# Block 0's prologue: the root per half on GpSimd, the silu table first, both halves' products ahead of later rounding, the order written down

## The chip, the cores and the metric

The kernel runs on one core of a Trainium2 chip. The core has five engines that run on their own and meet at semaphores: TensorE (PE) multiplies, VectorE (DVE) and ScalarE (ACT) work elementwise, GpSimd (POOL) does elementwise work on SBUF, and SyncE (SP) issues most of the transfers. The metric is device time in microseconds, lower is better.

## The reference

Two layers, one behind the other. The first is attention without a softmax: for each of 8 batches and 8 heads, `kv = k^T v` over 576 positions, then `out = q kv`, and each 64-wide row of `out` is divided by its root mean square and multiplied by `g_norm`. The second is a gated feed-forward layer over 4608 tokens of width 512, with an inner width of 1536.

```python
kv = np.einsum('bhsd,bhse->bhde', k, v)
out = np.einsum('bhsd,bhde->bhse', q, kv)
rms = np.sqrt(np.mean(out * out, axis=-1, keepdims=True) + 1e-06)
out = out / rms * g_norm                      # -> x, 4608 x 512
g = x @ w_gate
silu = g * (1.0 / (1.0 + np.exp(-g)))
return silu * (x @ w_val) @ w_out
```

Inputs `q`, `k`, `v` and the output are float32; the three weight matrices arrive as 64-bit numbers, read as pairs of 32-bit words, and are made into float32 on the chip.

## The kernel before

The tokens are worked in nine blocks of 512. For each block, an `Att` object turns `q`, multiplies it by the `kv` of its batch, takes the root mean square, scales and turns the result into `x` (features on partitions); an `Ffn` object makes the gate and value products, `h = silu(g) * v`, and the down product. Blocks 1 to 8 use products with fewer multiplications, whose extra operands VectorE and GpSimd make; block 0 uses plain products (`plain_up`, twelve steps f = 0 to 11, each with four gate and four value matrix products), since its weights are still arriving.

The weights come in 36 pieces of 512 KB: gate and value in turn, twelve each, then twelve of `w_out`. A piece is a `Words` object. It is loaded into one of four buffers named `ld` by an SP transfer (L135). `begin` makes the magnitude of the high words on ScalarE (L146), clamps it (L147), masks out the sign (L152) and joins the two (L153), all three on VectorE; `finish` scales the low words on ScalarE (L160) and adds them in on VectorE (L162). `weights(n)` brings the count of rounded pieces to n, and each one asks for the load of a piece four ahead, which waits until a buffer is read out: by L152 and L160, the last readers of `raw`.

Block 0 starts in `first()`. The first two q tiles are turned on TensorE (L337) and copied out (L339 on ScalarE, L341 on VectorE); `first_kv` makes `kv` of batch 0 in two groups (L248) and copies and adds the banks (L253, L111); `heads` multiplies (L361); `squares` squares on ScalarE (L374) and sums on VectorE (L375). `root` takes the root of both halves in one go, on VectorE: a scaled sum (L381), a first guess from the bits (L384), and three refinement steps of three instructions each (L391 to L393). `warm` repeats a product that nobody reads, seven times (L496). `scale` multiplies a half by the root (L113), `turn_x` turns it on TensorE (L410) and copies it out with the gain on ScalarE (L411). A half is 256 tokens.

The order on each engine's queue comes from a scheduler that works through the program with costs and priorities; `tc.issue_after(x)` puts what stands under it behind instruction x. A queue is then worked strictly in that order. So a step that waits holds up what stands behind it on its engine.

After block 0's twelve steps, block 1's inputs are loaded by SP: `load_kv` (L266) and `load_q`, 32 small transfers (L284) into two `ld` buffers, once rounding has left these. VectorE turns q of block 1 (L331), and TensorE, after the first step of the down product (L565), multiplies it (L361). Silu is at L1040, the plain products at L1035.

Of the kernel before, what the change touches and what calls it, by code (L numbers as in the profile page):

```python
# [1 line left out]

# [16 lines left out]
def kernel(  # L19
# [41 lines left out]
    nc = tc.nc  # L61

    B, H, S, D = q.shape
# [7 lines left out]
    NS = DM // P  # L71
    NF = FF // P
# [3 lines left out]
    eps = 1e-6  # L76
# [6 lines left out]
    consts = pool("consts", 1)  # L83
    ld_pool = pool("ld", 4)
    st_pool = pool("st", 2)
# [26 lines left out]
    sub = lambda e, o, a, b: e.tensor_tensor(out=o, in0=a, in1=b, op=OP.subtract)  # L112
    mul = lambda e, o, a, b: e.tensor_tensor(out=o, in0=a, in1=b, op=OP.mult)  # L113

    def ring():

        return r_pool.tile([P, 4, BLK], F32, name="r")

    class Words:
# [12 lines left out]
        def __init__(self, src, shape):  # L132
            self.raw = ld_pool.tile([P, LD], U32, name="ld")[:, 0 : 2 * BLK]
            dst = self.raw.rearrange("p (a b) -> p a b", a=shape[0])
            self.sent = nc.sync.dma_start(out=dst, in_=src)  # L135
            self.shape = shape
            self.begun = False

        def begin(self):

            self.begun = True
            halves = self.raw.rearrange("p (f w) -> p f w", w=2)
            low, high = halves[:, :, 0], halves[:, :, 1]
            self.low, self.room = low, ring()
            mag = self.mag = self.room[:, 1].bitcast(U32)
            nc.scalar.activation(out=mag.bitcast(F32), in_=high.bitcast(F32), func=ACT.Abs)  # L146
            nc.vector.tensor_scalar(  # L147
                out=mag.bitcast(F32), in0=mag.bitcast(F32), scalar1=self.LOW, scalar2=self.HIGH,
                op0=OP.max, op1=OP.min,
            )  # L150
            sign = self.room[:, 2].bitcast(U32)
            nc.vector.tensor_scalar(out=sign, in0=high, scalar1=0x80000000, scalar2=None, op0=OP.bitwise_and)  # L152
            return nc.vector.scalar_tensor_tensor(  # L153
                out=mag, in0=mag, scalar=3, in1=sign, op0=OP.logical_shift_left, op1=OP.bitwise_xor
            )

        def finish(self, dst):

            unit = self.room[:, 0]
            nc.scalar.activation(out=unit, in_=self.low, func=ACT.Copy, scale=2.0**-51, bias=2.0)  # L160
# [32 lines left out]
    class Att:  # L193
# [128 lines left out]
                for r in range(2):  # L322
                    nc.scalar.copy(out=dst[:, r], in_=self.kv_ps[r])

        def turn_q(self, i, pools=None):

            if i == 0:
                self.qt = ring().rearrange("p j (t c) -> p t j c", t=T)
            if self.quarters:
                to = self.qt[:, :, 2 * i : 2 * i + 2].rearrange("p t j c -> p j t c")  # L330
                self.q_turned = nc.vector.transpose(out=to.rearrange("p j t c -> p (j t c)"), in_=self.q[i])  # L331
                return
            for t in (2 * i, 2 * i + 1):
                pool = pools[t % 2] if pools else m_psum
                ps = pool.tile([P, NS, P], F32, name=pool.name[0])
                for j in range(NS):
                    nc.tensor.transpose(ps[:, j], self.q[t][:, j], ident)  # L337
                if t % 2 if self.n == 0 else t:
# [127 lines left out]
        def first(self):  # L466
            self.turn_q(0, (b_psum, c_psum))
            self.first_kv(0, (b_psum, c_psum))
            last = self.first_kv(1, (b_psum, a_psum))

            with tc.issue_after(last.ins):
                self.heads(0, (0, 1), (m_psum, m_psum))
            with tc.issue_after(self.multiplied.ins):
                self.heads(0, (2, 3))
            self.squares(0)
            with tc.issue_after(self.multiplied.ins):
                self.turn_q(1, (b_psum, c_psum))

            with tc.issue_after(self.copied_q.ins), tc.issue_after(self.summed.ins):
                begun = words[pieces[0]].begin()  # L480
            with tc.issue_after(begun.ins):
                self.product(1, (b_psum, a_psum))
            self.warm()
            self.root(0, 2)
            self.scale(0)
            with tc.issue_after(self.squared.ins), tc.issue_after(self.scaled.ins):
                weights(1)
            self.turn_x(0)
            self.scale(1)
            return self.squared, self.scaled  # L490

        def warm(self):

            ps = c_psum.tile([P, NS, P], F32, name="c")
            for _ in range(7):
# [446 lines left out]
    class Ffn:  # L942
# [82 lines left out]

        def plain_up(self, f, halves=(0, 1)):

            if 0 in halves:
                self.ps[f] = [pool.tile([P, 2, HB], F32, name=pool.name[0]) for pool in (b_psum, c_psum)]
            of = slice(halves[0], halves[-1] + 1)  # L1030
            ps = [t[:, of] for t in self.ps[f]]
            x = self.att.x[:, 0:4].rearrange("p (h m) i t -> p (m i) h t", h=2)
            for t, w in zip(ps, (wg, wv)):
                for i in range(NS):
                    nc.tensor.matmul(  # L1035
                        t, lhsT=w[f // 2][:, i, P * (f % 2) : P * (f % 2 + 1)], rhs=x[:, i, of],
                        start=(i == 0), stop=(i == NS - 1),
                    )
            h = self.h[:, f].rearrange("p (h t) -> p h t", h=2)[:, of]
            nc.scalar.activation(out=h, in_=ps[0], func=ACT.Silu)  # L1040
            mul(nc.vector, h, h, ps[1])
# [37 lines left out]
    blocks[0].load_q(1)  # L1079
    load_weights(4)  # L1080
    squared, scaled = blocks[0].first()

    for n in range(NB):
        ffn = Ffn(n, blocks[n])
        nxt = blocks[n + 1] if n + 1 < NB else None
        if n == 0:

            with tc.issue_after(squared.ins), tc.issue_after(scaled.ins):
                weights(2)
            ffn.plain_up(0, (0,))  # L1090
            copied = blocks[0].copied
            blocks[0].turn_x(1)
            for f in range(NF):
                with tc.issue_after(blocks[0].copied.ins if f else copied.ins):
                    weights(2 * (f + 2))
                ffn.plain_up(f) if f else ffn.plain_up(0, (1,))
            weights(len(pieces))
            pairs = wo.rearrange("p (j e) d -> p e j d", e=2)
            t2(pairs[:, 0, :, HD:DM], pairs[:, 1, :, HD:DM], pairs[:, 0, :, 0:HD])
            nxt.room = x_pool.tile([P, 3, 7, P], F32, name="xi").rearrange("p a b c -> p (a b c)")  # L1100

            with tc.issue_after(sent.ins):
                for i in range(2):
                    nxt.load_kv(i)
                for i in range(2):
                    nxt.load_q(i)
            ffn.plain_end()
            for g in range(2):
                nxt.kv(g)
        else:  # L1110

            def visit(g):
                with tc.issue_after(ffn.multiplied.ins):
                    nxt.kv(g)
                if nxt.n < B:
                    ffn.visited = nxt.positions

            def third():
                visit(0)
# [12 lines left out]
            ffn.up(fill)  # L1132
# [48 lines left out]
```

## Time and profile before

| what | us |
|---|---|
| median of 3 runs (1021.38 to 1022.99) | 1022.85 |
| profiled execution | 1020.91 |
| its span, first to last instruction | 1019.1 |
| TensorE busy | 1003.5 |
| VectorE busy | 700.9 |
| GpSimd busy | 368.9 |
| ScalarE busy | 228.1 |

The span is what the trace covers; the profiled execution's own time is 1.8 us more. An engine's busy time counts its instructions, not its waits. TensorE is busy nearly all the time, and the chain that ended last runs over it for 90% of the span; VectorE holds 6% of that chain, transfers 2%, ScalarE 1%. The start of this chain, in order of time (start, length, what):

```profile
0.74 4.10 DMA h<-in_k_dram
4.85 0.02 issue
4.86 0.37 SPq L230
5.23 0.04 issue
5.28 7.74 DMA h<-in_v_dram
13.02 0.14 issue
13.15 0.37 PE b L248 x2
```

The first group's k and v arrive by 10 us and the second group's v at 13.02; until then loads set the pace. What the change touches lies behind that.

### The profile page before, as it was taken

The page shows a single profiled execution, that of the slowest core. Times are in us where ns is not written, and L with a number is a line of the kernel's source. Part 1 is how long each engine was busy: PE and PEld are TensorE (multiplying, and loading weights), DVE is VectorE, ACT ScalarE, POOL GpSimd, SP SyncE. Part 2 cuts the span into 40 slices and gives each one's busy share as a digit, 9 for nine tenths or more (in the row PEclk, how much of TensorE's full clock was granted, in tenths as well). Part 3 has the DMA queues.
Part 4 walks back from the last instruction along what each step waited for, and adds up shares of the span by engine and source line. Part 5 has one row for each costly group of instructions (what it writes and reads, how often), then busy time and mean ns, then how long its engine had stood idle before and what let it go on. Part 6 is the DMA issues. An engine that isn't in the chain of part 4 may idle for free.

```text
span 1019.1 us, 21397 instructions
## 1 busy us (share of the span) xinstructions
PE 1003.5 (98%) x8522; PEld 895.9 (88%) x8522; DVE 700.9 (69%) x1169; ACT 228.1 (22%) x353; POOL 368.9 (36%) x280
## 2 busy tenths in 40 slices
PE   6999999999999999999999999999999999999998
PEld 4544688888999899998999899988998999989997
DVE  3999688998666946685558566665668466946661
ACT  2765112121211221221121111111121211221110
POOL 0000263534055503561246315630555045513670
PEclk9999999999999999999999999999999999999999
DMA  8689643767888277846685568646772766066601
GB/s 238 202 257 273 119 81 109 188 165 159 251 231 244 50 195 202 248 83 147 206 234 136 101 207 241 168 62 194 233 201 44 182 191 192 22 169 199 194 25 42
DMA packets 273844, 170.26 MB, mean 167 GB/s; under 512 B 150608, under 2 KB 241872, under 8 KB 273744
## 3 DMA queue, kind: packets, MB, share of 16 engines
q1 hardware_dynamic: 238800, 164.42, 59.1%
q10 hardware_dynamic: 34880, 4.46, 2.7%
q8 instruction: 68, 1.11, 0.5%
q14 instruction: 32, 0.26, 0.1%
q0 software_dynamic: 64, 0.00, 0.0%
HBM read 138.02 MB, written 22.41 MB: 157 GB/s over the span
## 4 chain that ended last, share of the span: by engine, by line
PE 90%; DVE 6%; DMA 2%; issue 1%; ACT 1%; SPq 0%; DVEq 0%; ACTq 0%
PE b L728 26%; PE b L565 19%; PE c L728 13%; PE c L565 10%; PE a L728 6%; PE a L565 5%; PE b L1035 4%; PE c L1035 4%; PE m L361 1%; PE m L316 1%; DVE r L112 1%; DVE r L111 1%; DVE xi L112 1%; DMA h<-in_v_dram 1%; DVE t L112 1%
## 5 line engine op out<-in xcount | busy, mean ns | idle before, releaser
L111 POOL TENSOR_TENSOR r<-r 128x256 f32<-128x256 f32 (+1 forms) x105 | 110.7, 1061 | 295.2 <-DVE r L111 292.9
L111 DVE TENSOR_TENSOR r<-b,r 128x512 f32<-128x512 f32 (+1 forms) x273 | 161.9, 605 | 64.9 <-PE b L728 60.4
L112 POOL TENSOR_TENSOR t<-wo 128x512 f32<-128x512 f32 x81 | 114.4, 1436 | 211.9 <-DVE wo L111 102.6
L111 DVE TENSOR_TENSOR r<-c,r 128x512 f32<-128x512 f32 (+1 forms) x179 | 108.3, 616 | 89.1 <-PE c L728 58.2
L728 PE MATMUL b<-x,t 128*128 128x128 f32 x1092 | 151.2, 275 | 0.0
L111 DVE TENSOR_TENSOR r<-a,r 128x512 f32<-128x512 f32 (+1 forms) x99 | 62.4, 630 | 113.1 <-PE a L565 71.2
L728 PEld LDWEIGHTS b<-x,t 128*128 128x128 f32 x1092 | 136.5, 192 | 0.8 <-DVE r L111 0.2
L728 PE MATMUL c<-xi,t 128*128 128x128 f32 x840 | 112.4, 275 | 1.0 <-DVE xi L111 1.0
L113 POOL TENSOR_TENSOR h<-r 128x1024 f32<-128x1024 f32 (+1 forms) x40 | 82.4, 2075 | 82.2 <-DVE r L111 79.2
L728 PEld LDWEIGHTS c<-xi,t 128*128 128x128 f32 x840 | 102.9, 192 | 1.2 <-DVE xi L111 1.2
L565 PE MATMUL b<-wo,h 128*128 128x256 f32 x432 | 100.1, 383 | 0.1
L565 PE MATMUL b<-t,h 128*128 128x256 f32 x432 | 96.2, 379 | 0.0
L565 PEld LDWEIGHTS b<-t,h 128*128 128x128 f32 x432 | 82.0, 190 | 11.3 <-issue 0.2
L565 PEld LDWEIGHTS b<-wo,h 128*128 128x128 f32 x432 | 79.8, 190 | 13.2 <-DVE h L113 2.5
L742 ACT COPY r<-b 128x512 f32<-128x512 f32 x63 | 36.9, 585 | 214.9 <-PE b L728 208.1
L728 PE MATMUL b<-xi,t 128*128 128x128 f32 x588 | 79.7, 276 | 0.0
L728 PEld LDWEIGHTS b<-xi,t 128*128 128x128 f32 x588 | 72.4, 192 | 0.0
L728 PE MATMUL b<-x,wg 128*128 128x128 f32 x336 | 52.8, 279 | 0.2 <-DVE x L112 0.2
L728 PE MATMUL b<-x,wv 128*128 128x128 f32 x336 | 51.2, 275 | 0.0
L565 PE MATMUL a<-wo,h 128*128 128x256 f32 x216 | 48.3, 379 | 0.0
L565 PE MATMUL c<-t,s 128*128 128x256 f32 x216 | 48.1, 379 | 0.0
L565 PE MATMUL c<-wo,h 128*128 128x256 f32 x216 | 48.1, 379 | 0.0
(133 smaller groups left out, 1562.2 us busy)
## 6 DMA issues: line engine op xcount, KB each, us to landing
t<-w SPq DMA_DIRECT2D x336, 256.0 KB, 3.5
out_dram<-r SPq DMA_DIRECT2D x17, 512.0 KB, 3.1
ld<-in_k_dram SPq DMA_DIRECT2D x26, 288.0 KB, 4.9
ld<-in_v_dram SPq DMA_DIRECT2D x26, 288.0 KB, 5.8
ld<-in_moe_w_gate_dram SPq DMA_DIRECT2D x12, 512.0 KB, 4.7
ld<-in_moe_w_val_dram SPq DMA_DIRECT2D x12, 512.0 KB, 4.6
ld<-in_moe_w_out_dram SPq DMA_DIRECT2D x12, 512.0 KB, 5.0
w<-t SPq DMA_DIRECT2D x18, 256.0 KB, 3.0
```

The lines of the kernel that those rows point to most:

```text
L111: add = lambda e, o, a, b: e.tensor_tensor(out=o, in0=a, in1=b, op=OP.add)
L112: sub = lambda e, o, a, b: e.tensor_tensor(out=o, in0=a, in1=b, op=OP.subtract)
L113: mul = lambda e, o, a, b: e.tensor_tensor(out=o, in0=a, in1=b, op=OP.mult)
L316: self.positions = nc.tensor.matmul(self.kv_ps[r][u * D : (u + 1) * D, g, :], lhsT=k[:, u, c, :], rhs=v[:, u, c, :], start=(c == 0), stop= ...
L361: self.multiplied = nc.tensor.matmul(self.ps[i][u][p : p + D, t, j, :], lhsT=self.qt[rows, 2 * i + t, j, p : p + D], rhs=kvs[b % 3][rows, ...
L565: self.ffn.multiplied = nc.tensor.matmul(banks[e][:, e], lhsT=lhsT, rhs=rhs, start=first and i == 0 and (e == 0 or banks[0] is not banks[1 ...
L728: self.ffn.multiplied = nc.tensor.matmul(ps[:, i, f], lhsT=self.weight(o, p, f), rhs=self.operand(o, p), start=first and (i, f) == (0, 0), ...
L742: nc.scalar.copy(out=dst, in_=ps)
L1035: nc.tensor.matmul(t, lhsT=w[f // 2][:, i, P * (f % 2) : P * (f % 2 + 1)], rhs=x[:, i, of], start=(i == 0), stop=(i == NS - 1),)
```

## The change

The change rewrites block 0's prologue. Nine things are done:

- A small silu at the very start makes ScalarE load the silu's table there; the other functions used are in that table too, so the load ahead of the first real silu goes.
- `root` is no longer used by block 0. Each half has its own `inverse`: one VectorE instruction for the scaled sum, then GpSimd raises it to the power -0.5 with a constant tile `power`.
- `begin` is cut into `split` (magnitude, clamp, sign) and `join`; `scale` of the low words can be issued earlier. For the first two pieces VectorE masks the magnitude out as well, in place of ScalarE's L146.
- Both copies of the second pair of turned q tiles go to ScalarE.
- The second half's `heads` come before the first half's root is needed; `warm` has five repeats in place of seven.
- The first two pieces' steps are placed by hand between the halves' squares, sums and scales.
- TensorE's queue has half 0's gate and value products of f = 0, then half 1's turning, then half 1's products, where before the turning of half 1 was split around the value product.
- The third and fourth pieces (`weights(3)`, `weights(4)`) and the silus of f = 0 are put behind the last copy of x and the last scale.
- `in_order` writes the program's order down: each traced instruction of an engine is made to follow the one before it on that engine.

```diff
+    power = consts.tile([P, 4 * NS], F32, name="power")
+    nc.gpsimd.memset(power, -0.5)
+    early = consts.tile([P, 1], F32, name="early")
+    nc.vector.memset(early, 0.0)
+    nc.scalar.activation(out=early, in_=early, func=ACT.Silu)
...
         def begin(self):
             self.begun = True
+            self.split()
+            return self.join()
...
+        def split(self, engine=None):
...
+            if engine is nc.vector:
+                bits(sign, 0x80000000)
+                bits(mag, 0x7FFFFFFF)
+            else:
+                nc.scalar.activation(out=mag.bitcast(F32), in_=high.bitcast(F32), func=ACT.Abs)
...
         def first(self):
             self.turn_q(0, (b_psum, c_psum))
             self.first_kv(0, (b_psum, c_psum))
...
+            with in_order():
+                self.first_kv(1, (b_psum, a_psum))
                 self.heads(0, (0, 1), (m_psum, m_psum))
-            with tc.issue_after(self.multiplied.ins):
                 self.heads(0, (2, 3))
-            self.squares(0)
-            with tc.issue_after(self.multiplied.ins):
-                self.turn_q(1, (b_psum, c_psum))
-
-            with tc.issue_after(self.copied_q.ins), tc.issue_after(self.summed.ins):
-                begun = words[pieces[0]].begin()
-            with tc.issue_after(begun.ins):
-                self.product(1, (b_psum, a_psum))
-            self.warm()
-            self.root(0, 2)
-            self.scale(0)
-            with tc.issue_after(self.squared.ins), tc.issue_after(self.scaled.ins):
+                first.split(nc.vector)
+                self.square(0)
+                self.turn_q(1, (b_psum, c_psum), nc.scalar)
+                first.scale()
+                self.sum_squares(0)
+                self.inverse(0)
+                self.heads(1, range(NS), (b_psum, a_psum))
+                self.warm()
+                first.join()
+                self.square(1)
                 weights(1)
-            self.turn_x(0)
-            self.scale(1)
+                second.split(nc.vector)
+                second.scale()
+                self.sum_squares(1)
+                self.inverse(1)
+                self.scale(0)
+                self.turn_x(0)
+                second.join()
+                weights(2)
+                self.scale(1)
...
+        def inverse(self, i):
+            z, y = (x[:, i].rearrange("p u t j -> p (u t j)") for x in (self.z, self.y))
+            nc.vector.tensor_scalar(out=z, in0=z, scalar1=1.0 / D, scalar2=eps, op0=OP.mult, op1=OP.add)
+            nc.gpsimd.tensor_tensor(out=y, in0=z, in1=power, op=OP.pow)
...
-            for _ in range(7):
+            for _ in range(5):
...
         if n == 0:
-            with tc.issue_after(squared.ins), tc.issue_after(scaled.ins):
-                weights(2)
-            ffn.plain_up(0, (0,))
-            copied = blocks[0].copied
-            blocks[0].turn_x(1)
-            for f in range(NF):
-                with tc.issue_after(blocks[0].copied.ins if f else copied.ins):
+            with in_order(ffn_engine):
+                ffn.plain_products(0, (0,))
+                blocks[0].turn_x(1)
+                ffn.plain_products(0, (1,))
+            with tc.issue_after(blocks[0].copied.ins), tc.issue_after(scaled.ins), in_order():
+                weights(3)
+                ffn.plain_h(0, (0,))
+                weights(4)
+                ffn.plain_h(0, (1,))
+            for f in range(1, NF):
+                with tc.issue_after(blocks[0].copied.ins):
                     weights(2 * (f + 2))
-                ffn.plain_up(f) if f else ffn.plain_up(0, (1,))
+                ffn.plain_up(f)
```

More of the change, by code (lines that the diff above doesn't have):

```diff
@@ L1 @@
-from contextlib import ExitStack
+from contextlib import ExitStack, contextmanager
 import concourse.bass as bass
@@ L113, with in_order @@
     mul = lambda e, o, a, b: e.tensor_tensor(out=o, in0=a, in1=b, op=OP.mult)
+    power = consts.tile([P, 4 * NS], F32, name="power")
[3 more added lines that the diff above has]
+    nc.scalar.activation(out=early, in_=early, func=ACT.Silu)
+    @contextmanager
+    def in_order(*engines):
+        traced = nc.cur_bb.bb.instructions
+        last = traced[-1]
+        yield
+        start = next(k for k in reversed(range(len(traced))) if traced[k] is last) + 1
+        before = {}
+        for i in traced[start:]:
+            if engines and i.engine not in engines:
+                continue
+            if i.engine in before:
+                tc.add_manual_dep(
+                    i, before[i.engine].name,
+                    mybir.DependencyInfo(mybir.DependencyClass.NoSync, mybir.DependencyReason.DATA), reason="order",
+                )
+            before[i.engine] = i
     def ring():
@@ L136, in __init__ @@
             self.shape = shape
-            self.begun = False
+            self.begun = self.scaled = False
         def begin(self):
             self.begun = True
+            self.split()
+            return self.join()
+        def split(self, engine=None):
             halves = self.raw.rearrange("p (f w) -> p f w", w=2)
             low, high = halves[:, :, 0], halves[:, :, 1]
-            self.low, self.room = low, ring()
+            self.low, self.high, self.room = low, high, ring()
             mag = self.mag = self.room[:, 1].bitcast(U32)
-            nc.scalar.activation(out=mag.bitcast(F32), in_=high.bitcast(F32), func=ACT.Abs)
+            sign = self.room[:, 2].bitcast(U32)
+            bits = lambda to, mask: nc.vector.tensor_scalar(
+                out=to, in0=high, scalar1=mask, scalar2=None, op0=OP.bitwise_and
+            )
+            if engine is nc.vector:
[3 more added lines that the diff above has]
+                nc.scalar.activation(out=mag.bitcast(F32), in_=high.bitcast(F32), func=ACT.Abs)
             nc.vector.tensor_scalar(
@@ L150, in begin, with join @@
             )
-            sign = self.room[:, 2].bitcast(U32)
-            nc.vector.tensor_scalar(out=sign, in0=high, scalar1=0x80000000, scalar2=None, op0=OP.bitwise_and)
+            if engine is not nc.vector:
+                bits(sign, 0x80000000)
+        def join(self):
+            self.begun = True
+            mag, sign = (self.room[:, i].bitcast(U32) for i in (1, 2))
             return nc.vector.scalar_tensor_tensor(
@@ L155, in begin, with scale @@
             )
+        def scale(self):
+            self.scaled = True
+            nc.scalar.activation(out=self.room[:, 0], in_=self.low, func=ACT.Copy, scale=2.0**-51, bias=2.0)
         def finish(self, dst):
+            if not self.scaled:
+                self.scale()
             unit = self.room[:, 0]
-            nc.scalar.activation(out=unit, in_=self.low, func=ACT.Copy, scale=2.0**-51, bias=2.0)
             a, b = self.shape[0], BLK // self.shape[0]
@@ L323, in kv, with turn_q @@
                     nc.scalar.copy(out=dst[:, r], in_=self.kv_ps[r])
-        def turn_q(self, i, pools=None):
+        def turn_q(self, i, pools=None, engine=None):
             if i == 0:
@@ L337, in turn_q @@
                     nc.tensor.transpose(ps[:, j], self.q[t][:, j], ident)
-                if t % 2 if self.n == 0 else t:
+                if engine is nc.scalar or (t % 2 if self.n == 0 else t):
                     self.copied_q = nc.scalar.copy(out=self.qt[:, t], in_=ps)
@@ L468, in first @@
             self.first_kv(0, (b_psum, c_psum))
-            last = self.first_kv(1, (b_psum, a_psum))
-            with tc.issue_after(last.ins):
+            first, second = words[pieces[0]], words[pieces[1]]
+            self.z, self.y = (st_pool.tile([P, 2, 2, 2, NS], F32, name=x) for x in "zy")
+            self.sq = ring().rearrange("p f (t j d) -> p f t j d", t=2, j=NS)
+            with in_order():
+                self.first_kv(1, (b_psum, a_psum))
                 self.heads(0, (0, 1), (m_psum, m_psum))
-            with tc.issue_after(self.multiplied.ins):
@@ new lines, in first, with square @@
+                second.split(nc.vector)
[7 more added lines that the diff above has]
+                self.scale(1)
+            return self.squared, self.scaled
+        def square(self, i):
+            for u in range(2):
+                self.squared = nc.scalar.activation(out=self.sq[:, 2 * i + u], in_=self.ps[i][u], func=ACT.Square)
@@ new lines, in sum_squares @@
+        def sum_squares(self, i):
+            for u in range(2):
+                nc.vector.tensor_reduce(
+                    out=self.z[:, i, u], in_=self.sq[:, 2 * i + u], axis=mybir.AxisListType.X, op=OP.add
+                )
+        def inverse(self, i):
+            z, y = (x[:, i].rearrange("p u t j -> p (u t j)") for x in (self.z, self.y))
+            nc.vector.tensor_scalar(out=z, in0=z, scalar1=1.0 / D, scalar2=eps, op0=OP.mult, op1=OP.add)
+            nc.gpsimd.tensor_tensor(out=y, in0=z, in1=power, op=OP.pow)
@@ L1026, in plain_up, with plain_products @@
         def plain_up(self, f, halves=(0, 1)):
+            self.plain_products(f, halves)
+            self.plain_h(f, halves)
+        def plain_products(self, f, halves):
             if 0 in halves:
@@ L1034, in plain_up @@
                 for i in range(NS):
-                    nc.tensor.matmul(
+                    self.multiplied = nc.tensor.matmul(
                         t, lhsT=w[f // 2][:, i, P * (f % 2) : P * (f % 2 + 1)], rhs=x[:, i, of],
@@ L1038, in plain_up, with plain_h @@
                     )
+        def plain_h(self, f, halves):
+            of = slice(halves[0], halves[-1] + 1)
+            ps = [t[:, of] for t in self.ps[f]]
             h = self.h[:, f].rearrange("p (h t) -> p h t", h=2)[:, of]
@@ L1081 @@
     squared, scaled = blocks[0].first()
+    ffn_engine = blocks[0].multiplied.ins.engine
     for n in range(NB):
```

## The prediction, made before the changed kernel ran

> **What bounds the kernel now.** I read the page's first part, then the chain of waits, then the windows of busy time, and last the timelines of single engines around the two places where the chain and the change meet.
>
> ```profile
> PE 1003.5 (98%) x8522; PEld 895.9 (88%) x8522; DVE 700.9 (69%) x1169; ACT 228.1 (22%) x353; POOL 368.9 (36%) x280
> ```
>
> TensorE is busy for 98% of the span, so a gain can only come from its 15.6 us of idle time, about 10 of which lie before 34 us. The chain of waits, in order of time, shows what stands there:
>
> ```profile
> 21.99 1.20 DVE z L375 x2
> ...
> 25.68 1.30 DVE r L113 x2
> ...
> 30.79 1.28 ACT L1040
> ...
> 33.03 0.59 ACT x L411
> ...
> 33.66 1.99 PE b L1035 x8
> ```
>
> Between the first two lines lie the eleven small instructions of `root` (23.22 to 25.68); L1040 is the table load ahead of the first silu; at 33.66 the second half's product for f = 0 starts, and from there the chain stays on TensorE, without a gap, to the end of the down product's first step at 120.57. So the first place is "when does the line at 33.66 start".
>
> The second place is hidden in a chain that has no slack. Columns of the windows: stretch, length, busy time of each engine.
>
> ```profile
> 40.00:60.00 20.00, 20.00 (x48) 8.77 (x47) 20.00 (x43) 13.85 (x23) 0.00 (x0) 1.00 0.81 249
> 60.00:80.00 20.00, 20.00 (x48) 8.90 (x47) 20.00 (x43) 13.93 (x23) 0.00 (x0) 1.00 0.83 263
> ```
>
> VectorE, third figure after the length, is busy for 20.00 of 20.00 as well: the rounding of the 36 weight pieces runs at VectorE's pace. It ends near 101 us, and the profile's whole-span share of 69% doesn't show it. What hangs on it is in the timelines of VectorE, SP and TensorE (start, duration):
>
> ```profile
> 96.96 0.42 DVE L152 TENSOR_SCALAR r<-ld 128x512 uint32<-128x512 uint32 x1
> ```
> ```profile
> 97.44 20.23 SPq L284 DMA_DIRECT2D ld<-in_q_dram  x32
> ```
> ```profile
> 119.30 1.25 DVE L331 STREAM_TRANSPOSE r<-ld 128x1024 f32<-128x1024 f32 x1 [0.85 <-DMA ld<-in_q_dram]
> ```
> ```profile
> 115.12 5.45 PE L565 MATMUL b<-wo,h 128*128 128x256 f32 x24
> 120.50 0.27 PE L361 MATMUL m<-kv,r 64*64 64x64 f32 x1
> ```
>
> The L152 ends at 97.38 and frees a load buffer; 0.06 us later SP begins block 1's 32 q loads, which take 20.23 us; the second transpose of q waits for the last of them and ends at 120.55; block 1's products (L361) need it from their seventeenth matmul on, which comes about 0.28 us after 120.50, at 120.78. So in this execution SP's q chain and TensorE reach L361 with 0.15 us between them. A gain of TensorE before 115 us is kept only if the q chain moves earlier too, and a delay of the q chain goes straight into the time.
>
> **What the Trainium skill says.** "ScalarE: Activation LUTs", What ACT_TABLE_LOAD costs, gives about 1283 ns for a load and about 1380 ns more for a drain; the trace has the 1.28 us, and the silu starts at 32.08, right behind it, so I take no drain. "GPSIMD Engine Reference", section 3.1, puts a two-input elementwise operation at about 2.6 cycles an element and about half VectorE's rate; this trace has GpSimd at 1061 ns for 128x256 and 1436 ns for 128x512, thus about 1.46 ns an element on a floor near 0.69 us. It has no row for the power. "TensorE: Matmul & The Clock Gate", section What's actually happening, says that an idle window of about 3.4 us halves the array's clock and a busy one restores it. The four transposes at 17.20 took 396 ns each on average, those at 18.61 took 287: the trace shows both states, but no stall of more than 3.4 us after 21 us. Its section Architectural detail: the array is 16× 32×32, not 1× 128×128 says VectorE and ScalarE queues are strictly first in, first out, which the timelines fit.
>
> **The change part by part**, on the profiled execution (span 1019.1, its time 1020.91).
>
> *Up to 20.57: nothing.* The table load moves to the kernel's start, behind ScalarE's first load issue; its other three issues come some 1.6 us later (1.28 for the load, the rest for the small silu). They feed only the last step of each `first_kv`, at 10.1 and 13.1 us, and the loads took 4 to 5 us; SP's loads bind there. Bound: 0 to 0.3 us. The heads, the copies of the turned q (one goes from VectorE to ScalarE, which is free at 18.39) and the second heads stay: TensorE is through at 20.57, and the two squares at 20.69 and 21.19.
>
> *VectorE from 16 to 27.2.* New order, with start-to-start prices from the timeline (0.34 for a mask or clamp, 0.60 for a join, a finish, a reduction or a scale, 0.22 for a small one): three steps of `split` before 17.4; two reductions behind the first squares 17.92 to 19.15; z to 19.38; join to 19.98; finish behind ScalarE's scale of the low words (19.88 to 20.45), 20.50 to 21.10; second split 1.02, to 22.12; two reductions to 23.32; z to 23.6; scale of half 0 to 24.80 (26.89 before); join and finish 1.2, to 26.0; scale of half 1 to 27.2. GpSimd's power of half 0 has from 19.4 to 23.6, that of half 1 from 23.6 to 26.0. Its price: at least the 0.69 us floor, at most unknown; I take 1 to 2 us, hidden. Over 4.2 us it shows in full.
>
> *TensorE.* Half 0's transposes start at 25.05 instead of 27.11; five `warm` repeats (4.3 us) end at 24.9 and cover the wait as seven did. As before 1.41 us to the first product (the two copies of x are in this), 26.46; gate 1.83 and value 1.73 to 30.02, now without half 1's transposes between; these 0.93, to 30.95; the first copy of half 1 starts at 30.55 and ends at 31.13; the product that began at 33.66 starts at 31.27. That is 2.4 us won, from the root (2.0), and the table load and the rounding steps that sat ahead of the copies on ScalarE.
>
> *What is pushed behind.* ScalarE's queue now holds all four copies of x, and behind them the magnitude of the third weight piece (landed near 19 us; started at 28.93 before). The fourth copy ends at 31.7, the magnitude at 32.3. VectorE has nothing it may do between 27.2 and 32.3: 5.1 us idle, where it had none. Summed to the L152 that frees the buffer: VectorE starts at 16.2 instead of 18.23 (-2.0); its work changes by -2.0 for the root, -0.6 for the copy, +0.7 for two magnitudes, +0.6 for one more h product placed ahead of that L152, together -1.3; its idle time grows from 0.8 to some 6.3 (0.6 ahead of the first squares, 0.5 for the scaled low words, 5.1 here, 0.1 elsewhere), +5.5. So that L152 comes 2.2 us later, at about 99.6. Step by step through the queues I get the same: the fourth gate piece is done at 43.1 instead of 41.6, with 0.7 more left to do. In the tightest stretch, f = 1 and f = 2, the pieces are ready within 0.2 us of TensorE's need, so 0 to 0.5 us of stall there, which costs nothing in the end as TensorE waits later anyway.
>
> *The second place.* TensorE ends the down product's first step at 118.2. The q loads run 99.6 to 119.9, the second transpose ends at 122.75, and L361 goes on at 122.83, not 120.78: 2.05 us later than before. Behind it TensorE has no other waits of length, so the loss stays. **Forecast: span +2.05, the profiled time 1020.91 becomes 1022.96. The median of the runs shown is 1.94 above that execution, so 1024.9 us.** The own range of this step is +1.2 to +2.9, from 0.8 us of doubt in VectorE's idle time.
>
> **The rivals.**
> - *Slower by more, because TensorE's clock falls.* TensorE then stands still from 118.45 to 122.83, 4.4 us. If the clock falls, one to two windows of 3.4 us run at half speed: 1.7 to 3.4 us, an estimate from the named page. Time 1027.4. For: the stall is longer than a window. Against: the windows run free, and only about (4.4 - 3.4) / 3.4, three in ten, hold a whole idle one.
> - *Faster, because transfers and not VectorE pace the rounding.* The third pair of pieces is requested at about 20.5 and 22.3 (before: 22.36 and 29.51); if arrival of pieces sets the pace, the stream catches up its 2.2 us and the q loads begin 2.4 us earlier: 1020.4. For: DMA share 0.81 to 0.99, and 7.4 us of ScalarE's idle time behind w_out loads. Against: VectorE has no gap from 41 to 97 but one or two of 0.2 us, and SP waited 41.1 us for L152. It decides if the q loads begin before 97.4.
> - *No change.* The stream catches up some 2 us, or has less idle time: 1022.8.
> - *The power is slow*, 8 us or so: 3.8 us past its slack on everything, 1028.7. Nothing in the profile speaks for or against.
>
> **How the numbers follow.** Forecast 0.48, fallen clock 0.20, faster 0.15, no change 0.10, slow power 0.07. A measurement of this kernel can tell about 0.2%, 2.05 us, from no change; the forecast stands on that edge, so 0.25 of its 0.48 counts as slower and 0.23 as the same. Slower 0.25 + 0.20 + 0.07 = 0.52; same 0.23 + 0.10 = 0.33; faster 0.15. The range 1020.4 to 1027.5 leaves out the slow power, the upper part of the fallen clock and half of the faster case. The forecast's own range is 1024.0 to 1025.8.
>
> **What would show it.** Right: f = 0's second half starts near 31.3; VectorE idle some 5 us before 32.3; q loads near 99.6; TensorE idle about 4.4 us at 118.4. Wrong: q loads at or before 97.4; VectorE gaps between 45 and 97; a power longer than 4 us, which would put the first L113 behind GpSimd; a first `first_kv` that waits on ScalarE's loads.

## The result and the profile after

| | before | after |
|---|---|---|
| median of 6 runs, us | 1021.91 (1020.93 to 1022.99) | 1025.08 (1023.82 to 1026.93) |
| profiled execution, us | 1020.91 | 1026.93 |
| its span, us | 1019.1 | 1025.2 |
| TensorE's mean granted clock over the runs | 0.998 to 1.000 | 0.996 to 0.998 |

(The clock of before is from its 27 executions beside the first experiments; it was 1.000 in nearly all of them and 0.998 in two.) The change makes the kernel slower by 3.2 us: the ratio is 1.0031, with a 95% interval of 1.0018 to 1.0044. The profiled execution of after is the slowest of its six, so the differences below are a little larger than the usual ones.

The page's busy times look as before:

```profile
PE 1003.2 (98%) x8518; PEld 896.6 (87%) x8518; DVE 701.0 (68%) x1162; ACT 226.1 (22%) x352; POOL 379.1 (37%) x283
```

TensorE is busy for 0.3 us less in a span that is 6.1 us longer. It has two unread products fewer, and some of its work ran slowly, as will be seen. First the start. TensorE's timeline of after, from the first turning of x on (start, duration, what, count, and in brackets the idle time before and what ended it):

```profile
25.76 1.09 PE L458 MATMUL m<-ident,r 128*128 128x128 f32 x8
27.20 1.99 PE L1110 MATMUL b<-x,wg 128*128 128x256 f32 x8 [0.34 <-ACT x L459]
29.03 1.89 PE L1110 MATMUL c<-x,wv 128*128 128x256 f32 x8
30.75 1.04 PE L458 MATMUL m<-ident,r 128*128 128x128 f32 x8
32.13 1.99 PE L1110 MATMUL b<-x,wg 128*128 128x256 f32 x8 [0.34 <-ACT x L459]
```

The second half's product starts at 32.13; before it was 33.66. The start has become shorter, by 1.5 us here. GpSimd's two powers, and VectorE after its last scale:

```profile
20.71 3.23 POOL L560 TENSOR_TENSOR y<-z,power 128x16 f32<-128x16 f32 x1 [17.67 <-DVE z L559]
24.59 2.90 POOL L560 TENSOR_TENSOR y<-z,power 128x16 f32<-128x16 f32 x1 [0.65 <-DVE z L559]
```
```profile
27.53 0.69 DVE L113 TENSOR_TENSOR r<-b,y 128x512 f32<-128x512 f32 x1 [0.39 <-POOL y L560]
28.14 0.68 DVE L113 TENSOR_TENSOR r<-a,y 128x512 f32<-128x512 f32 x1
33.24 0.43 DVE L184 TENSOR_SCALAR r<-r 128x512 f32<-128x512 f32 x1 [4.42 <-ACT r L183]
```

VectorE waits 0.39 us for the second power, and then 4.42 us for ScalarE's magnitude (L183) of the third weight piece. ScalarE had nothing to do for 3.67 of these, but its queue held half 1's copies of x ahead of the magnitude:

```profile
31.39 1.26 ACT L459 ACTIVATE x<-m,gain 128x512 f32<-128x512 f32 x2 [3.67 <-PE m L458]
32.55 0.66 ACT L183 ACTIVATE r<-ld 128x512 f32<-128x512 f32 x1
```

From 40 to 80 us VectorE has next to no idle time again (third figure after the length), so what it lost ahead of 33 us it does not win back:

```profile
40.00:60.00 20.00, 20.00 (x48) 8.66 (x47) 19.88 (x43) 12.82 (x22) 0.00 (x0) 1.00 0.82 257
60.00:80.00 20.00, 20.00 (x48) 8.88 (x47) 20.00 (x43) 13.70 (x24) 0.00 (x0) 1.00 0.81 259
```

Now the second place, in the timelines of SP, VectorE and TensorE:

```profile
101.23 21.12 SPq L332 DMA_DIRECT2D ld<-in_q_dram  x32
```
```profile
123.99 1.25 DVE L379 STREAM_TRANSPOSE r<-ld 128x1024 f32<-128x1024 f32 x1 [5.90 <-DMA ld<-in_q_dram]
```
```profile
113.81 5.45 PE L635 MATMUL b<-wo,h 128*128 128x256 f32 x24
125.29 0.36 PE L409 MATMUL m<-kv,r 64*64 64x64 f32 x1 [5.41 <-DVE r L379]
128.06 6.71 PE L635 MATMUL b<-wo,h 128*128 128x256 f32 x24
134.61 5.34 PE L635 MATMUL c<-t,s 128*128 128x256 f32 x24
```

Before, at the same three points (L361 leaves 128 records here; after stands still ahead of the thirty-third, so that one is shown):

```profile
121.01 0.22 PE L361 MATMUL m<-kv,r 64*64 64x64 f32 x1
122.52 5.45 PE L565 MATMUL b<-wo,h 128*128 128x256 f32 x24
127.81 5.34 PE L565 MATMUL c<-t,s 128*128 128x256 f32 x24
```

The q loads begin 3.8 us later than before (97.44), the second transpose comes 4.7 us later (119.30), and TensorE, which reached the down product 1.3 us earlier (113.81, before 115.12), stands still for 5.41 us. Behind the wait it is slow: a down step of 24 matmuls takes 6.71 us where the one ahead of it took 5.45. The windows show why; the third figure from the end is the granted clock (first before, then two lines of after):

```profile
121.00:126.00 5.00, 5.00 (x127) 4.55 (x117) 4.57 (x9) 2.30 (x5) 0.00 (x0) 1.00 1.05 235
```
```profile
121.00:126.00 5.00, 0.71 (x26) 0.71 (x30) 2.01 (x2) 0.00 (x0) 0.00 (x0) 0.78 0.57 127
126.00:140.00 14.00, 14.00 (x129) 12.30 (x126) 12.82 (x25) 2.75 (x5) 4.19 (x3) 0.83 0.69 148
```

So the profiled execution adds up as follows, each against before at the same point. The heads go on at 125.29 instead of 121.01, +4.28. From there to the second down step it takes 2.77 us instead of 1.51, +1.26, and that step, start to start, 6.55 instead of 5.29, +1.26: the low clock costs 2.5 us. That makes +6.80 at 134.61; the spans differ by 6.1. The missing 0.7 comes back before 245 us, where block 1's third down step of this kind starts 6.1 us later than before (244.48 and 238.37).

### The profile page after: what moved, and what is told of

It reads as the page before. It is cut to its first block, busy times and chain, and to the rows that moved or that the text cites. A ratio compares the mean times of both kernels' runs of the same rounds, so it can differ in the third digit from the quotient of the medians.

```text
span 1025.2 us, 21386 instructions
## 1 busy us (share of the span) xinstructions
PE 1003.2 (98%) x8518; PEld 896.6 (87%) x8518; DVE 701.0 (68%) x1162; ACT 226.1 (22%) x352; POOL 379.1 (37%) x283
## 4 chain that ended last, share of the span: by engine, by line
PE 85%; DVE 8%; DMA 3%; SPq 1%; issue 1%; ACT 1%; DVEq 0%; ACTq 0%
PE b L798 26%; PE b L635 20%; PE c L798 13%; PE c L635 10%; PE a L798 6%; PE a L635 5%; PE m L409 2%; SPq L332 1%; PE m L364 1%; DVE r L195 1%; DVE r L112 1%; DVE xi L112 1%; DMA h<-in_v_dram 1%; DMA ld<-in_v_dram 1%; DVE r L111 1%; PE b L1110 1%
## 5 line engine op out<-in xcount | busy, mean ns | idle before, releaser
L112 POOL TENSOR_TENSOR t<-wo 128x512 f32<-128x512 f32 x81 | 117.9, 1478 | 188.3 <-DVE wo L111 81.3
```

## The experiments

Theory: VectorE's 4.4 us of idle time, made by ScalarE's order, delays block 1's q chain; the chain's wait and the clock that falls in it cost more than the start gains. Rivals: the loss lies elsewhere, the transfers set the chain's pace, or the clock costs nothing that counts. The median of the kernel before beside these runs was 1021.7 to 1022.1.

**The q loads on two queues, on the changed kernel and on the one before.**

```diff
-                            nc.sync.dma_start(
+                            (nc.scalar if self.n == 1 and r % 2 else nc.sync).dma_start(
                                 out=to[32 * r : 32 * (r + 1), j, g0:g1],
```

> The changed kernel; of block 1's 32 q loads, every second group of four heads' quarters is issued on ScalarE's queue instead of SP's. Theory (the loss is block 1's q chain): the loads begin near 101 as in the changed kernel but take about 11 us instead of 21, the second transpose of q is done near 115, TensorE goes from its first matmuls on 128x64 heads at 119.2 straight into the second half, no stall of 5.4 us and no slow clock behind it. The time is the kernel before less TensorE's lead of 1.3 us at that place: 1020.6 us, within 0.6. Rival 1 (the q loads are paced by the transfers, not by the issuing queue): they still take about 20 us and the time stays near 1025. Rival 2 (the loss lies elsewhere, later in the kernel): the stall goes and the time stays above 1023.

> The kernel before with the same split of block 1's q loads over two queues. Theory: the kernel before had 0.15 us between the q chain and TensorE and so waits for nothing there; the split frees a chain that doesn't decide: 1021.9 us, within 0.4. Rival: in most executions the kernel before waits there too, and the split alone is worth 1 us or more: 1021 or less.

Measured: 1018.15 us (1017.54 to 1019.72), ratio to before 0.9962 (0.995 to 0.9974), and on the kernel before 1022.16 (1021.09 to 1022.81), ratio 1.000 (0.9992 to 1.0008). The same edit is worth 6.9 us on one kernel and nothing on the other. In the changed kernel SP's half takes 11.81 us where all 32 took 21.12, so the issuing queue paces these loads. The stall is gone:

```profile
31.20 1.99 PE L1110 MATMUL b<-x,wg 128*128 128x256 f32 x8 [0.34 <-ACT x L459]
```
```profile
112.88 5.45 PE L635 MATMUL b<-wo,h 128*128 128x256 f32 x24
120.53 5.45 PE L635 MATMUL b<-wo,h 128*128 128x256 f32 x24
125.81 5.34 PE L635 MATMUL c<-t,s 128*128 128x256 f32 x24
```

It came out 2.4 us below what I expected. About 0.9 of that is TensorE's lead, which I had taken from the profiled execution of after: here the second half's product starts at 31.20, and the first down step at 112.88, 2.2 us ahead of before instead of 1.3. Some 0.7 is won between 122 and 245 us, as told below. The rest lies within the 1.1 us by which the profiled execution of before is faster than the median beside this run.

**The third and fourth pieces ahead of half 1's copies.** ScalarE gets their four instructions where it was idle, and VectorE their rounding up to the join.

```diff
+            ahead = lambda: [f() for k in pieces[2:4] for f in (words[k].begin, words[k].scale)]
-            with in_order(ffn_engine):
-                ffn.plain_products(0, (0,))
-                blocks[0].turn_x(1)
+            with in_order(ffn_engine, squared.ins.engine), ExitStack() as behind:
+                ffn.plain_products(0, (0,)); behind.enter_context(tc.issue_after(blocks[0].copied.ins)); ahead()
+                behind.close(); blocks[0].turn_x(1)
                 ffn.plain_products(0, (1,))
```

> The changed kernel; ScalarE's magnitude and scaling of the third and fourth weight pieces stand between its copies of x for half 0 and those for half 1 (four instructions, about 2 us, in ScalarE's idle time from 27.2 to 31), and VectorE's steps of these pieces may follow. q loads as in the changed kernel. Theory (VectorE's 4.4 us of idle time before 33.2 is what makes the q loads late): the idle time falls to 1 us or less, the rounding stream runs about 3.5 us earlier, the q loads begin near 97.7 instead of 101.2, TensorE does not stall or stalls under 1 us at its second half of block 1's heads: 1020.6 to 1021.5 us. Rival (transfers of weights and of k and v set the stream's end, DMA engines being busy for 0.96 of 80 to 100 us): the q loads begin at 100 or later all the same, and the time stays above 1023.5.

Measured: 1017.76 us (1017.00 to 1018.91), ratio 0.9957 (0.9946 to 0.9969): faster than both kernels. VectorE, SP and TensorE in this kernel:

```profile
30.39 0.42 DVE L176 TENSOR_SCALAR r<-ld 128x512 uint32<-128x512 uint32 x1
32.24 0.43 DVE L184 TENSOR_SCALAR r<-r 128x512 f32<-128x512 f32 x1 [1.42 <-ACT r L183]
```
```profile
95.22 19.43 SPq L332 DMA_DIRECT2D ld<-in_q_dram  x32
```
```profile
112.58 5.45 PE L635 MATMUL b<-wo,h 128*128 128x256 f32 x24
119.98 5.45 PE L635 MATMUL b<-wo,h 128*128 128x256 f32 x24
125.27 5.34 PE L635 MATMUL c<-t,s 128*128 128x256 f32 x24
```

The idle time falls from 4.42 to 1.42 us and the q loads begin at 95.22, with all 32 still on SP. The idle time is thus the cause, not a companion, and the transfers do not hold the stream's end at 100 us.

**The third piece alone.** The same edit with `pieces[2:3]`.

> As the kernel with the pieces ahead, but the third piece alone stands ahead of half 1's copies of x, not the fourth. Theory (the time follows VectorE's idle time in small steps): of VectorE's 4.4 us idle time about 2 us is filled, the q loads begin about 2 us earlier than in the changed kernel, near 98 (over the executions seen so far those began at 99.0 to 101.2), the second transpose of q ends within 1 us of TensorE's coming to it, near 118.5 to 119.5, and the clock stays: 1018.8 us, within 0.7. Rival (half a shift is not enough: a short wait still drops the clock): 1020 to 1021.5, with a mean clock of 0.998 to 0.999.

Measured: 1024.58 us (1019.91 to 1027.25), ratio 1.0023 (1.0013 to 1.0033): no help that shows. The expectation failed, for a reason that VectorE's timeline gives:

```profile
27.77 0.69 DVE L195 SCALAR_TENSOR_TENSOR r<-r 128x512 uint32<-128x512 uint32 x1
32.83 0.69 DVE L210 CUSTOM_DVE_ANT_0 wg<-r 128x1024 uint16<-128x1024 uint16 x1 [4.37 <-PE b L1110]
```
```profile
100.20 6.00 SPq L332 DMA_DIRECT2D ld<-in_q_dram  x9
```

The third piece's finish writes the second half of a `wg` tile whose first half TensorE is still reading, for f = 0; it waits 4.37 us for that product, and the queue behind it with it. The idle time is as long as in the changed kernel, only its place has moved, and so the q loads begin at 100.20 (the line is cut where the window ends). With two pieces ahead, the steps of the fourth piece and those of the fifth up to its join stand ahead of this finish in VectorE's timeline; there it comes at 33.52 and waits for nothing. This kernel's executions also spread widely. Of 18, the one whose mean clock stayed at 1.000 took 1019.91 us, the six at 0.998 took 1020.73 to 1024.44, and the eleven at 0.996 or 0.997 took 1024.00 to 1027.25.

**Unread matmuls in the wait.** A first try put five of 128x512 between the two halves of block 1's heads, with the second turned q tile among what they read:

```diff
-                self.ps[i] = [pool.tile([P, 2, NS, D], F32, name=pool.name[0]) for pool in pools]
+                self.ps[i] = [pool.tile([P, 2, NS, D], F32, name=pool.name[0]) for pool in pools]; (self.n, i) == (1, 1) and self.warm(5, 1)
...
+                nc.tensor.matmul(ps, lhsT=ident, rhs=self.qt[:, of], start=True, stop=True)
```

> The changed kernel with five matmuls of 128x512 (about 0.85 us each, results unused) on TensorE between the first and the second half of block 1's heads, where it stands still for 4.4 to 5.4 us. They end at about 123.5, before or near the second transpose of q, so the stall itself is not shortened. Theory (the stall also costs about 2 us because TensorE's clock falls in it and comes back only some 3 us later): the granted clock stays at 1.00 behind the stall and the time falls by about 2 us: 1023.0 us, within 0.7. Rival (the clock's fall costs nothing that counts, all of the loss is the wait): 1025.1, or more where the five matmuls end after the transpose.

Measured: 1028.71 us (1026.70 to 1030.35), ratio 1.0058 (1.0042 to 1.0075). They read a part of q that only the second transpose makes, so they came behind the wait and not into it:

```profile
123.58 0.36 PE L409 MATMUL m<-kv,r 64*64 64x64 f32 x1 [4.62 <-DVE r L379]
125.07 6.50 PE L566 MATMUL c<-r,ident 128*128 128x512 f32 x10
132.36 5.45 PE L635 MATMUL b<-wo,h 128*128 128x256 f32 x24
```

As a test of the theory it is void. The second try reads the part that is there, and stands ahead of the heads:

```diff
-                self.product(0, (m_psum, a_psum))
+                self.n == 1 and self.warm(5, self.qt[:, 0:2, 0:2]); self.product(0, (m_psum, a_psum))
```

> The changed kernel with the five matmuls of 128x512 (4.3 us together at full clock, results unused; they read only the part of q that the first transpose has made) ahead of the first of block 1's heads, right behind the down product's first step. The wait for the second transpose of q stays, but it shrinks from 4.4 to 5.4 us to about 1 us. Theory (the wait costs its length and, because the clock falls in it, some 2 us behind it): the granted clock is 1.00 from 121 to 140 us, the matmuls of heads take 0.22 us and not 0.31 behind the wait, and the time falls by 1.5 to 2.5 us: 1023.0. Rival (the clock's fall is no loss that counts): 1025.1.

Measured: 1022.38 us (1021.46 to 1023.59), ratio 1.0004 (0.9996 to 1.0012), clock 0.999 or 1.000 in all 13 executions. TensorE's timeline and window:

```profile
112.27 5.45 PE L635 MATMUL b<-wo,h 128*128 128x256 f32 x24
117.56 4.45 PE L566 MATMUL c<-r,ident 128*128 128x512 f32 x10
123.97 5.45 PE L635 MATMUL b<-wo,h 128*128 128x256 f32 x24
```
```profile
121.00:126.00 5.00, 5.00 (x140) 3.96 (x139) 3.36 (x5) 2.06 (x4) 0.00 (x0) 1.00 1.06 260
```

4.45 us of work that nobody reads make the changed kernel 2.7 us shorter (1025.08 to 1022.38), near the 2.5 us that the trace of after showed. In this execution the second transpose was done at 120.79 and the matmul that needs it started at 122.46, so the last 1.6 us or so of the five were too much.

**The table load.** Three kernels move it: behind ScalarE's four load issues in the changed kernel; not early at all in the changed kernel; not early at all where the q chain is free.

```diff
-    nc.scalar.activation(out=early, in_=early, func=ACT.Silu)
...
-    blocks[0].load_first_kv()
+    blocks[0].load_first_kv(); nc.scalar.activation(out=early, in_=early, func=ACT.Silu)
```

> The changed kernel; the early silu, and with it ScalarE's table load, stands behind ScalarE's four load issues instead of behind the first one. Theory (the three loads that the table load delays make the first stage late): the second part of block 0's k-v products starts near 13.2 instead of 14.5, TensorE and VectorE are 0.6 us earlier from 21 us on, the q loads begin 0.6 us earlier, and the time falls by 0.6 to 1.2: 1024.2 us. Rival (the late start is a spread between executions): no change, 1025.1 us, and the start varies with no relation to the order.

> The changed kernel without the early silu and nothing else: ScalarE loads silu's table (1.28 us) ahead of the first silu, behind the third piece's magnitude and scaling. Theory (the early load's worth lies in VectorE's stream alone, which sets the q loads): VectorE waits 1.0 to 1.3 us longer near 35, the q loads begin near 102.3, TensorE's stall grows by as much: 1026.2 us, within 0.8. Rival (VectorE's later waits for w_out pieces, or slack, take it in): 1025.1, within 0.5, as it was with the q chain relieved.

The first takes both edits of the diff, the second only the first one. Measured: 1024.59 us (1020.47 to 1026.84), ratio to before 1.0015 (1.0003 to 1.0027), and 1025.62 (1021.58 to 1027.12), ratio 1.0036 (1.0026 to 1.0046). Neither stands apart from the changed kernel's 1025.08. The start alone varies by more: with the table load where the change puts it, VectorE's first scaled sum (L559) came at 20.38 in after and at 18.51 to 19.34 in five other kernels, and the two of this experiment, at 19.95 and 18.81, lie between. In the kernel without the early load VectorE waits 0.45 us for ScalarE behind the first silu, not the 1.0 to 1.3 that I expected.

**The three edits together, and from there the root and the table.** The first kernel has the two queues, both pieces ahead and the table load behind the load issues. The second then does each half's root by VectorE's ten instructions, in place of the power:

```diff
-            nc.gpsimd.tensor_tensor(out=y, in0=z, in1=power, op=OP.pow)
+            steps(z, y, st_pool.tile([P, 2, 2, 2, NS], F32, name="a")[:, i].rearrange("p u t j -> p (u t j)"))
```

The third has no early silu.

> The changed kernel with three edits together: third and fourth piece ahead of half 1's copies, block 1's q loads on two queues, the early silu behind ScalarE's load issues. Theory: the first two free the same chain, and either alone leaves TensorE without a wait there, so they do not add: 1017.5 us, within 0.6, the same as with the pieces ahead alone. Rival (the q chain, or VectorE's stream behind it, still holds TensorE up in part with one of them alone): 1016.5 or less.

> As the kernel with the three edits, but the root of each half by VectorE's ten small instructions (one estimate, three steps of three) in place of GpSimd's power. Theory (the power takes VectorE's root off the path to the first product): ten instructions of 0.22 us per half stand ahead of the scale of half 0, less the 0.4 us that VectorE now waits for the power of half 1: half 0's scale 4 us later, the second half's first product near 35.3 instead of 31.2, and the time 4 us longer than with the three edits, 1021.5 us, up to 2 us more if TensorE's clock falls in its longer wait. Rival (VectorE's idle time before 32 takes the root in for nothing): within 1 us of the three edits.

> As the kernel with the three edits, but without the early silu: the table for silu is loaded (1.28 us) ahead of the first silu of the first feed-forward column, near 32, as in the kernel before. Theory (all four copies of x now stand ahead of the first silu, so the load is off the path to the second half's product; it delays only the rounding of later pieces, which has slack with the q loads on two queues): within 0.5 us of the three edits, 1017.7. Rival (TensorE takes the pieces for f = 1 and 2 within 0.2 us of their being ready, so the 1.28 us delays it): 1018.8 us, with waits of TensorE for wg or wv between 34 and 45.

Measured: 1017.82 us (1017.53 to 1018.29), ratio 0.9954 (0.994 to 0.9969); with VectorE's root 1023.86 (1021.81 to 1025.34), ratio 1.0018 (1.0011 to 1.0025); with the late table 1018.06 (1017.76 to 1018.57), ratio 0.9956 (0.9943 to 0.9969). So either relief of the q chain is enough, the early table load is worth 0.2 us there, which is within the spread, and the power is worth 6.0 us in this order of things. About 4 of them are the instructions (twice ten, 2.1 us for each half) and about 1.5 the clock; for the last 0.5 I have no line. The profiled execution of the kernel with VectorE's root is the fastest of its 22 and only 4.1 us above that of the three edits. TensorE's timeline in it shows the longer wait and the slow product behind it:

```profile
27.68 1.09 PE L458 MATMUL m<-ident,r 128*128 128x128 f32 x8 [4.17 <-DVE r L113]
29.11 3.47 PE L1110 MATMUL b<-x,wg 128*128 128x256 f32 x8 [0.34 <-ACT x L459]
...
35.53 2.00 PE L1110 MATMUL b<-x,wg 128*128 128x256 f32 x8 [0.34 <-ACT x L459]
```

The five `warm` products no longer cover the wait, and after 4.17 us of it the first gate product takes 3.47 us instead of 2.0.

## Why the prediction was right, and where its sizes were off

The direction, the mechanism and the two places were right: the start is shorter, the rounding stream is later, and block 1's q chain turns that into a loss. The experiments show each link: fill VectorE's idle time, or quicken the q loads, and the loss becomes a gain of 4 us.

- *Up to 20.57, nothing.* Right on average, with a spread between executions that I had not reckoned with: after's own profile is some 1 us late at this point (20.38 where I had z at 19.38), five others with the same start lie at 18.5 to 19.3. That the table load makes it late was not shown.
- *The second half's product at 31.27.* 32.13 in the profiled execution, and between 30.57 and 31.20 in six others whose start is the same or lacks only the early load. The 2.4 us are confirmed.
- *The power, 1 to 2 us, hidden.* It took 3.23 and 2.90 us. Half 0's stayed within the slack that I had given it; half 1's showed by 0.4 us.
- *VectorE idle for 5.1 us.* 4.42, and 0.39 ahead of it for the power; the reason was as written.
- *q loads from 99.6, for 20.2 us.* 101.23 for 21.12 us in the profiled execution; between 98.96 and 101.13, for 18 to 19 us, in five others that lose as much on VectorE ahead of 36 us and leave the loads on SP. Part of the profiled lateness is its late start; VectorE also waits twice for ScalarE near the stream's end, 0.38 us at 96.72 and 0.61 at 101.77; before it did so once, for 0.54.
- *L361 goes on at 122.83.* 125.29, and between 121.50 and 123.83 in four others that waited.
- *0.15 us between the q chain and TensorE, and 2.05 us of loss.* The reading of L361 was off. All five executions that wait do so before the thirty-third record; the trace has two records for each matmul of the program, so that is the seventeenth matmul. Before, it starts at 121.01, not at 120.78. The slack was thus about 0.4 us, and the forecast's own steps give 122.83 less 121.01, a loss of 1.8 us.
- *The clock.* The step that failed. I had it as a rival with a chance of 0.20, on the ground that only a window of 3.4 us that is wholly idle would count. By the mean clock it fell in every execution of after (0.996 to 0.998), and in the profiled execution of the kernel without the early load it fell behind a wait of only 2.44 us. It costs about 2.5 us on top of the wait, so the rival was no alternative to the forecast but a second term of it. Its size had been put well, at 1.7 to 3.4 us. The two states that the prediction saw in the transposes at 17.20 and 18.61 rest on their lengths alone; the clock recorded there is 1.00 at both.

The forecast difference was 2.05 us and the measured one is 3.17. That 1024.9 still lies 0.2 from the measured 1025.08 is luck: the clock's cost was left out, and against it the three runs of before that I started from had a median 0.94 above that of all six. Also, after and three other kernels of this start (two queues, pieces ahead, second try of unread matmuls) win 0.6 to 0.7 us between 122 and 245 us (with the pieces ahead the lead is 2.54 us at 119.98 and 3.13 at 235.24). With the three edits it is only 0.2 us, and with the late table 0.2 are lost there. I have not tested what gives these 0.6 us.

Not tried: a separate tile for each half of `wg`, which would let the third piece finish early without the fourth one's help; and the written order (`in_order`) taken out by itself, so what it alone is worth stays open.

## What to carry to other kernels

When an order is written out by hand, go through each queue and ask what now stands behind an instruction that waits: here one engine's free 3.7 us became another's idle 4.4, and its price was paid 90 us later, in a load chain with 0.4 us to spare. Count a stall of the matrix engine of a few microseconds with its clock, not with its length alone. And price a gain at the next place where its engine has to wait for somebody else: what was won at the start became worth something only once that place was freed.

## What was not expected of the hardware

- The clock falls sooner than at a whole window of idleness. "TensorE: Matmul & The Clock Gate", section What's actually happening, of the Trainium skill puts the fall after one or more idle windows of about 3.4 us. Here it fell behind 2.44 us; the wait and the windows of the kernel without the early load:

```profile
121.50 0.27 PE L409 MATMUL m<-kv,r 64*64 64x64 f32 x1 [2.44 <-DVE r L379]
```
```profile
121.00:126.00 5.00, 4.50 (x102) 4.06 (x103) 4.74 (x7) 2.17 (x4) 0.00 (x0) 0.66 1.01 237
126.00:140.00 14.00, 14.00 (x66) 12.32 (x66) 13.52 (x23) 0.58 (x1) 7.72 (x6) 1.00 0.74 141
```

  Cut finer, the clock of this kernel is 1.00 through the whole wait and 0.50 from 122.1 to 125.5. In all six profiled executions in which it fell behind a wait, it stood at 0.50 for 3.41 us (three of them) or for 6.83 us (the other three, after among them, from 123.8 to 130.7).
- GpSimd's power of 128x16 takes 3.23 us the first time and 2.90 or 2.91 the second, in all ten traces that have it; the same work as ten VectorE instructions takes 2.1 us (0.21 each).
- 32 small loads on one queue took 18.0 to 21.1 us in eight kernels, about 0.6 us each; on two queues they took 12.8 us from the first issue to the end of the last (101.66 to 114.47).
